# Attention and two MLP layers in one kernel: key and query loads behind the leftover scores, GpSimd's operations behind VectorE's

## The chip, the cores and the metric

The kernel runs on one core of one Trainium2 chip. A core has five engines, each with its own instruction stream, worked off in order: TensorE (PE, matrix products), VectorE (DVE), ScalarE (ACT), GpSimd (POOL) and SyncE (SP), which here issues most of the DMAs. The metric is the device time of one execution, in microseconds (us); less is better.

## The reference

Three stages follow each other. Attention works with sigmoid in place of softmax; its output, with the heads side by side, is the input of a first MLP layer, and that one's output the input of a second, gated one.

```python
def _attn_ref(q, k, v):                     # (4, 12, 448, 64) each
    S = q.shape[2]
    scores = np.matmul(q, k.transpose(0, 1, 3, 2)) / np.sqrt(64) - np.log(S)
    attn = 1.0 / (1.0 + np.exp(-scores))
    return np.matmul(attn, v)

def _moe_ref(x, w_in, w_out):               # x (1792, 768), 768 -> 2048 -> 768
    h = x @ w_in
    return (h - np.tanh(h)) @ w_out

def _moe2_ref(x, w_gate, w_val, w_out):     # 768 -> 1536 -> 768
    gate = 1.0 / (1.0 + np.exp(-(x @ w_gate)))
    return (gate * (x @ w_val)) @ w_out
```

All inputs and the output (1792 x 768) are float32.

## The kernel before

**Attention** goes over 24 pairs of heads (NP = 24). The loop (L3119 and following) makes one iteration per pair p, and in each the engines' instructions are written down in this order:

- `scores(p)`: PE's score products, sa (L2351), from the split keys and queries, each followed by a sigmoid on ScalarE (L2355);
- `split(p + 1)`: six VectorE operations (L2300 to L2309) that split the next pair's keys kt and queries qt into a high and a low part, tile sp; at its end, before the change, `load(p + 4)`, four DMAs of 112 KB from SP (L2266);
- `pair_time()`: a planner fills the other engines' time with work for the MLP layers (below), and issues that work's DMAs on SP;
- `load_v(p + 2)`: the values, one DMA from SP (L2275) and four small ones from GpSimd's own stream (L2277, L2282), tile vt;
- `values(p - 1)`: PE's products of the scores with the values, pv (L2392, L2378), and their eviction to x by ScalarE (L2401); after pairs 5 and 11 a store of x, xs (L2403);
- `rest()`: the leftover scores sl of pair p (L2336), four products per pair that read kt and qt themselves, and their sigmoid al on ScalarE (L2340).

Keys and queries lie in four buffers. `load(p + 4)` writes into the buffer of pair p, whose last reader is `rest()` of pair p, so these DMAs wait for PE's leftover scores. SP issues its DMAs in order over eight semaphores in turn: a DMA is issued only when the one eight places before it has landed.

**The planner.** Weights are loaded as packed integers (st, L1686), decoded by ScalarE and VectorE (mw or ms; the decoding of a part starts with an Abs on ScalarE, L1717, or on VectorE), and some decoded ones are stored for later use (kept, L1795). VectorE, ScalarE and GpSimd convert them into high and low parts (w, w_t, w_b), some of which are stored too (half_t, half_b, L1889). The MLP's matrix products go by a scheme of seven products over sums of blocks; their left operands (a11, s1, s2, a12, s3, s4, a22) are made in attention from the first blocks of x (x0, x1), by casts on VectorE and by sums on both VectorE and GpSimd. All these operations stand on line L1346 in the profile, that of a helper. Each is a task with a due time; the planner goes along with clocks of its own for each engine (`busy`, `now`) and puts each operation of a task on the engine and into the pair where its reckoning ends first. Its time is negative in attention, from -5.38 * 23 = -123.7 to 0. Where it puts an operation on GpSimd at a time over 0, it has it wait for the last VectorE operation that its reckoning ends by then:

```python
            if e == "g" and t > 0:
                before = next((ins for over, ins in reversed(marks) if over < t + 0.05), None)
                if before is not None:
                    tc.add_manual_dep(
                        gpsimd.last.ins, before.ins.name, IN_TURN, reason="shared SBUF port"
                    )
```

`marks` holds the operations that the planner has put on VectorE. The order of instructions on an engine is the order in which they are written; nothing is rearranged afterwards.

**The MLP layers** follow attention on PE: products pa, pb, pc, pe (L2791) of the first layer's first half, then pq (L2497), and so on.

Of the kernel before, what the change touches and what calls it, by code (L numbers as in the profile page):

```python
# [1352 lines left out]
def fast_path(  # L1353
# [134 lines left out]
    class Task:  # L1488
# [66 lines left out]
        def go(self, at):  # L1555
            kinds, f, _, _, lock = self.ops[self.at]
            end, t, e = at
            if e == "s":
                end = moved(t, kinds[e])
                busy[e] = t + 0.4  # L1560
            else:
                busy[e] = end
            if lock:
                busy["l"] = end
            self.end.append(end + SHOW)
            self.at += 1
            if self.done():
                tasks.remove(self)
            elif self.dues:
                self.due = self.dues[self.at]  # L1570
                tasks.sort(key=lambda t: t.due)
            f(ENGINE[e]) if "g" in kinds else f(e) if "a" in kinds and "v" in kinds else f()
            mark(e)
            if e == "g" and t > 0:
                before = next((ins for over, ins in reversed(marks) if over < t + 0.05), None)
                if before is not None:
                    tc.add_manual_dep(
                        gpsimd.last.ins, before.ins.name, IN_TURN, reason="shared SBUF port"
                    )
# [707 lines left out]
    def split(p):  # L2287

        if p >= NP:
            return  # L2290
        qt, kt = qk_t.pop(p)
        t = qkp.tile([128, 2 * KR + QGAP + 2 * S], F32R, tag="sp", name=f"sp{p}", bufs=2)
        kk = t[:, :2 * KR].rearrange("p (i c r) -> p i c r", i=2, r=128)
        qq = t[:, 2 * KR + QGAP:].rearrange("p (i s) -> p i s", i=2)
        parts = (
            (kt[:, :KR - (NCH - 1) * EX].rearrange("p (c r) -> p c r", r=CP), slice(0, CP)),
            (kt[:, (NCH - 1) * CP:KR].rearrange("p (c r) -> p c r", r=EX), slice(CP, 128)),
        )
        for src, r in parts:
            nc.vector.tensor_copy(out=kk[:, 0, :, r], in_=src)  # L2300
        if p == 0:
            nc.scalar.activation(out=qq[:, 0], in_=qt, func=AF.Copy)
        for src, r in parts:
            nc.vector.tensor_tensor(
                out=kk[:, 1, :, r], in0=src, in1=kk[:, 0, :, r].bitcast(F32), op=ALU.subtract
            )
        if p:
            nc.vector.tensor_copy(out=qq[:, 0], in_=qt)
        nc.vector.tensor_tensor(out=qq[:, 1], in0=qt, in1=qq[:, 0].bitcast(F32), op=ALU.subtract)  # L2309
        s_t[p] = kk, qq, kt, qt  # L2310
        load(p + 3)

    slots = [0]

# [781 lines left out]
    with tc.manual_schedule():  # L3096
# [11 lines left out]
        for _ in range(10):  # L3108
            nc.tensor.matmul(pz[:, :S], z[:, :128], z, start=True, stop=True)
        split(0)  # L3110

        first = list(first_jobs)

# [9 lines left out]
        for p in range(NP - 1):  # L3123
            if p == TUNE.get("p0", 2):
                for i, job in enumerate(first):
                    create(job, BEGIN + TUNE.get("c0", 16.0) + gap * (i + 1))
            if p == NP // 2 + 1:
                src_at[0] = now[0] + 6.0
                prepare(0, TUNE.get("x0", -40.0), 6.0)
            rest = scores(p)  # L3130
            split(p + 1)
            pair_time()
            if p:
                load_v(p + 2)
                values(p - 1)
                rest()
        p = NP - 1
        scores(p)
        rest_keys(p - 1)
# [260 lines left out]
```

## Time and profile before

| | |
|---|---|
| time, median of 3 runs | 1067.13 us (1066.64 to 1069.18) |
| the profiled execution | 1068.06 us, of which the span 1066.3 us |
| PE busy | 1043.1 us, 98% of the span |
| VectorE busy | 825.0 us, 77% |
| ScalarE busy | 592.3 us, 56% |
| GpSimd busy | 306.2 us, 29% |
| mean granted clock of PE | 0.993 of full speed |
| DMA engines | 264.56 MB, mean 248 GB/s |

The span runs from the first to the last instruction of one profiled execution; times within the trace count from its start. An operation is named by its output and its input (out<-in, without buffer numbers) and by its line. "Idle before, releaser" in a row of the timeline is the time for which the engine stood before the operation, and what it waited for last. The clock is that which the chip granted to PE, as a share of full speed.

### The profile page before, as it was taken

What the parts mean: (1) busy time and instruction counts of PE and PEld (TensorE: products, weight loads), DVE (VectorE), ACT (ScalarE), POOL (GpSimd) and SP (SyncE); (2) the same over time, 40 slices, a digit from 0 to 9 for tenths busy, and PEclk for the clock granted to TensorE, in tenths of its full rate; (3) what the DMA queues carried; (4) which work ended last, traced back from release to release, by engine and by line L of the source; (5) the groups of instructions that cost most, each with busy time, mean ns of one, the idle gap of its engine ahead of it and who ended that gap; (6) DMA issues with size and microseconds to landing.
All of it is one profiled execution on the core that took longest, in us unless ns stands there. A gap on an engine that the chain in (4) does not pass through costs nothing.

```text
span 1066.3 us, 16297 instructions
## 1 busy us (share of the span) xinstructions
PE 1043.1 (98%) x5913; PEld 937.6 (88%) x5913; DVE 825.0 (77%) x1380; ACT 592.3 (56%) x970; POOL 306.2 (29%) x328
## 2 busy tenths in 40 slices
PE   9989899999999999999999999999999999999996
PEld 5756578989999999999999998999999999999996
DVE  5979997898776899956879999867665888534577
ACT  6756567586467677654677545644334544314343
POOL 5446634524111323121233112352113011016103
PEclk9989999999999999999999999999999999999999
DMA  8998469974463455995557858849777465996312
GB/s 226 272 284 259 130 209 389 374 276 183 159 257 117 186 198 178 334 423 213 219 219 324 317 200 298 333 179 359 269 274 285 179 238 224 395 404 225 133 75 105
DMA packets 63539, 264.56 MB, mean 248 GB/s; under 512 B 8672, under 2 KB 24032, under 8 KB 59360
## 3 DMA queue, kind: packets, MB, share of 16 engines
q1 hardware_dynamic: 59792, 260.40, 66.3%
q0 software_dynamic: 3072, 2.17, 0.9%
q8 instruction: 48, 0.79, 0.3%
q10 hardware_dynamic: 592, 0.92, 0.3%
q14 instruction: 35, 0.29, 0.1%
HBM read 162.40 MB, written 101.06 MB: 247 GB/s over the span
## 4 chain that ended last, share of the span: by engine, by line
PE 90%; DVE 6%; ACT 1%; issue 1%; DMA 1%; POOL 0%; SPq 0%; ACTq 0%; POOLq 0%; DVEq 0%
PE pq L2497 33%; PE pa L2791 13%; PE pb L2791 13%; PE pc L2791 13%; PE pe L2791 7%; PE pv L2392 4%; PE sa L2351 4%; DVE y L1346 1%; PE pv L2378 1%; PE pq_b L2558 1%; PE pq_c L2558 1%; PE sl L2336 1%; PE pq_a L2558 1%; DVE mw L1346 1%; DMA kept<-mw 1%
## 5 line engine op out<-in xcount | busy, mean ns | idle before, releaser
L2497 PE MATMUL pq<-gg,w 128*128 128x448 f32 x1800 | 382.5, 362 | 0.7 <-ACT y L2506 0.7
L2497 PEld LDWEIGHTS pq<-gg,w 128*128 128x128 f32 x1800 | 337.0, 187 | 25.0 <-ACT y L2506 1.1
L1346 DVE TENSOR_TENSOR y<-pq,y 128x448 f32<-128x448 f32 x195 | 120.4, 620 | 57.5 <-PE pq L2497 56.3
L2791 PE MATMUL pa<-a,w_b 128*128 128x448 f32 x720 | 157.3, 362 | 1.0 <-DVE sg L1346 1.0
L2791 PEld LDWEIGHTS pa<-a,w_b 128*128 128x128 f32 x720 | 134.8, 187 | 10.6 <-DVE sg L1346 1.3
L1346 DVE SCALAR_TENSOR_TENSOR mw<-st,mw 128x768 int32<-128x768 int32 x104 | 100.5, 966 | 1.7
L2791 PE MATMUL pc<-s,w_t 128*128 128x448 f32 x360 | 78.7, 362 | 0.2 <-ACT pc L2812 0.2
L2791 PE MATMUL pb<-s,w_t 128*128 128x448 f32 x360 | 78.7, 363 | 0.0
L2791 PE MATMUL pb<-s,w_b 128*128 128x448 f32 x360 | 78.5, 362 | 0.0
L2791 PE MATMUL pe<-s,w_t 128*128 128x448 f32 x360 | 78.5, 362 | 0.0
L2791 PE MATMUL pc<-a,w_t 128*128 128x448 f32 x360 | 78.5, 362 | 0.0
L1346 POOL TENSOR_TENSOR gg<-sg,gg 128x448 fp32r<-128x448 f32 x38 | 43.6, 1159 | 109.8 <-DVE gg L1346 30.3
L1346 POOL TENSOR_TENSOR w<-mw,w 128x384 fp32r<-128x384 f32 x35 | 36.0, 1045 | 131.9 <-ACT w L1869 62.4
L1346 POOL TENSOR_TENSOR w_t<-mw,w_t 128x384 fp32r<-128x384 f32 x37 | 38.1, 1039 | 124.6 <-DVE w_t L1346 45.2
L2355 ACT ACTIVATE at<-sa,bias_s 128x896 f32<-128x896 f32 x72 | 67.2, 1008 | 10.1 <-PE sa L2351 7.8
L2791 PEld LDWEIGHTS pc<-s,w_t 128*128 128x128 f32 x360 | 67.3, 187 | 5.4 <-ACT pc L2812 0.9
L2791 PEld LDWEIGHTS pb<-s,w_t 128*128 128x128 f32 x360 | 67.2, 187 | 5.2 <-issue 0.3
L2791 PEld LDWEIGHTS pb<-s,w_b 128*128 128x128 f32 x360 | 67.5, 187 | 4.5
L2791 PEld LDWEIGHTS pe<-s,w_t 128*128 128x128 f32 x360 | 67.5, 188 | 4.5
L2791 PEld LDWEIGHTS pc<-a,w_t 128*128 128x128 f32 x360 | 67.5, 187 | 4.5
L1346 DVE TENSOR_SCALAR mw<-mw 128x768 f32<-128x768 f32 x104 | 60.4, 581 | 6.4 <-ACT mw L1717 5.0
L2351 PE MATMUL sa<-sp 64*128 64x448 f32 x432 | 52.8, 381 | 10.8 <-ACT al L2340 5.1
(148 smaller groups left out, 1624.2 us busy)
## 6 DMA issues: line engine op xcount, KB each, us to landing
half_t<-w_t SPq DMA_DIRECT2D x40, 768.0 KB, 4.6
w_t<-half_t SPq DMA_DIRECT2D x40, 768.0 KB, 6.7
st<-in_w_out_dram SPq DMA_DIRECT2D x28, 768.0 KB, 6.0
mw<-kept SPq DMA_DIRECT2D x22, 768.0 KB, 5.8
half_b<-w_b SPq DMA_DIRECT2D x20, 768.0 KB, 3.9
w_b<-half_b SPq DMA_DIRECT2D x20, 768.0 KB, 6.3
st<-in_w_in_dram SPq DMA_DIRECT2D x16, 768.0 KB, 6.1
kept<-mw SPq DMA_DIRECT2D x12, 768.0 KB, 4.2
```

What stands on the lines that cost most here:

```text
L1346: self.last = call(*args, **kw)
L2336: nc.tensor.matmul(pl[h * KL:(h + 1) * KL, j, :SH], kt[r, KR:], qt[r, h * SH:(h + 1) * SH], start=True, stop=True,)
L2351: nc.tensor.matmul(pa[:, j, :S], kk[r, ki, c], qq[r, qi], start=(i == 0), stop=(i == 2),)
L2355: nc.scalar.activation(out=at[:, :, c], in_=pa[:, :, :S], func=AF.Sigmoid, bias=bias_s, scale=qk_scale,)
L2378: nc.tensor.matmul(po[j * D:(j + 1) * D, h, :SH], vt[r, j, NCH - 1], al[r, j], start=not last, stop=last,)
L2392: nc.tensor.matmul(po[j * D:(j + 1) * D, h, :SH], vt[:, j, c], at[:, j, c, h * SH:(h + 1) * SH], start=(c == 0 and not rest_first), stop=( ...
L2497: nc.tensor.matmul(po[:, :S], wk[use, j][:, a, d], gt[t][:, c, j], start=i == 0 and not seeded, stop=i == 5, skip_group_check=seeded,)
L2558: nc.tensor.matmul(o, w[:, a, h * KH + d], move[x](b), start=fresh and i == 0, stop=i == 2, skip_group_check=not fresh,)
L2791: nc.tensor.matmul(bank[term], w[:, i, half * KH + c], t[:, j, c], start=fresh and at == 0, stop=at == 3 * KH - 1, skip_group_check=not fresh,
```

## The change

Two things change. First, the loads of keys and queries no longer stand at the end of `split`. `load(3)` comes once after the first split, and `load(p + 4)` at the end of iteration p, behind `rest()`, whose leftover scores free the buffer. Second, the wait of a GpSimd operation for VectorE's operations is now put in at planner times over -100 (TUNE has no entry "gt"), which takes in attention from its fifth pair on.

```diff
--- before.py
+++ after.py
@@ -1571,7 +1571,7 @@
                 tasks.sort(key=lambda t: t.due)
             f(ENGINE[e]) if "g" in kinds else f(e) if "a" in kinds and "v" in kinds else f()
             mark(e)
-            if e == "g" and t > 0:
+            if e == "g" and t > TUNE.get("gt", -100.0):
                 before = next((ins for over, ins in reversed(marks) if over < t + 0.05), None)
                 if before is not None:
                     tc.add_manual_dep(
@@ -2308,7 +2308,6 @@
             nc.vector.tensor_copy(out=qq[:, 0], in_=qt)
         nc.vector.tensor_tensor(out=qq[:, 1], in0=qt, in1=qq[:, 0].bitcast(F32), op=ALU.subtract)
         s_t[p] = kk, qq, kt, qt
-        load(p + 3)
 
     slots = [0]
 
@@ -3108,6 +3107,7 @@
         for _ in range(10):
             nc.tensor.matmul(pz[:, :S], z[:, :128], z, start=True, stop=True)
         split(0)
+        load(3)
 
         first = list(first_jobs)
 
@@ -3134,6 +3134,7 @@
                 load_v(p + 2)
                 values(p - 1)
                 rest()
+            load(p + 4)
         p = NP - 1
         scores(p)
         rest_keys(p - 1)
```

SP is the one engine whose instructions come in another order. Its DMAs around the store of a decoded weight, kept0_1_0, in iterations 9 and 10 (kt13 and qt13 are the keys and queries of pair 13, st00_4 a packed weight, vt11 the values of pair 11), before:

```order
L2266 DMA kt13_858<-in_k_dram 64x448 x2
L2266 DMA qt13_859<-in_q_dram 64x448 x2
L1686 DMA st00_4_866<-in_w_in_dram 128x1536
L2275 DMA vt11_870<-in_v_dram 112x2x192
L2266 DMA kt14_933<-in_k_dram 64x448 x2
L2266 DMA qt14_934<-in_q_dram 64x448 x2
L1795 DMA kept0_1_0_942<-mw0_1_791 128x1536
L1686 DMA st00_5_944<-in_w_in_dram 128x1536
L2275 DMA vt12_950<-in_v_dram 112x2x192
```

and now:

```order
L1686 DMA st00_4_860<-in_w_in_dram 128x1536
L2275 DMA vt11_864<-in_v_dram 112x2x192
L2266 DMA kt13_894<-in_k_dram 64x448 x2
L2266 DMA qt13_895<-in_q_dram 64x448 x2
L1795 DMA kept0_1_0_936<-mw0_1_785 128x1536
L1686 DMA st00_5_938<-in_w_in_dram 128x1536
L2275 DMA vt12_944<-in_v_dram 112x2x192
L2266 DMA kt14_974<-in_k_dram 64x448 x2
L2266 DMA qt14_975<-in_q_dram 64x448 x2
```

In each pair the weight's DMAs and the values now stand ahead of the four loads of keys and queries; pair 14's stand behind kept0_1_0 instead of ahead of it.

GpSimd keeps its order, but its operations get other waits (DVE_49 is a wait for VectorE, Pool_49 one for GpSimd itself, PE_49 one for PE, DMAHW and DMASW ones for landings). Around the values of pair 19, before:

```order
L1346 TENSOR_TENSOR s1_0_1329<-x1_88,s1_0_1329 128x448 [waits DVE_49]
L1346 TENSOR_TENSOR a12_0_1252<-x0_87,a12_0_1252 128x448
L1346 TENSOR_TENSOR a12_0_1252<-x0_87,a12_0_1252 128x448 [waits DVE_49]
L2277 DMA vt19_1489<-in_v_dram 16x3x64 [waits DMAHW5_49,DMASW4_49,PE_49]
L2277 DMA vt19_1489<-in_v_dram 16x3x64 [waits DMASW5_49]
L2282 DMA vt19_1489<-in_v_dram 64x2x64 [waits DMASW6_49]
L2282 DMA vt19_1489<-in_v_dram 64x2x64 [waits DMASW7_49]
L1346 TENSOR_TENSOR x1_88<-x0_87 128x448 [waits Pool_49] x2
L2277 DMA vt20_1564<-in_v_dram 16x3x64 [waits DMAHW4_49,DMASW0_49,PE_49]
```

and now:

```order
L1346 TENSOR_TENSOR s1_0_1323<-x1_88,s1_0_1323 128x448 [waits DVE_49]
L1346 TENSOR_TENSOR a12_0_1246<-x0_87,a12_0_1246 128x448 [waits DVE_49]
L1346 TENSOR_TENSOR a12_0_1246<-x0_87,a12_0_1246 128x448
L2277 DMA vt19_1483<-in_v_dram 16x3x64 [waits DMAHW1_49,DMASW4_49,PE_49]
L2277 DMA vt19_1483<-in_v_dram 16x3x64 [waits DMASW5_49]
L2282 DMA vt19_1483<-in_v_dram 64x2x64 [waits DMASW6_49]
L2282 DMA vt19_1483<-in_v_dram 64x2x64 [waits DMASW7_49]
L1346 TENSOR_TENSOR x1_88<-x0_87 128x448 [waits DVE_49,Pool_49]
L1346 TENSOR_TENSOR x1_88<-x0_87 128x448 [waits Pool_49]
L2277 DMA vt20_1558<-in_v_dram 16x3x64 [waits DMAHW0_49,DMASW0_49,PE_49]
```

The sums x1<-x0 waited for GpSimd's own earlier operations alone; the first of them now also waits for VectorE, for the last weight operation ahead of split 20. The second row's wait is on VectorE's cast of a12 ahead of split 19.

## Rows read from the trace of the kernel before

**Rows 1.** Page, part 1: engine, busy us, share of the span, instructions.
```profile
PE 1043.1 (98%) x5913; PEld 937.6 (88%) x5913; DVE 825.0 (77%) x1380; ACT 592.3 (56%) x970; POOL 306.2 (29%) x328
```

**Rows 2.** Stretches: length, busy us of PE, PEld, DVE, ACT, POOL, PEclk, DMA share, GB/s.
```profile
14.37:67.84 53.47, 53.47 (x585) 37.56 (x580) 47.80 (x101) 38.81 (x50) 25.24 (x41) 1.00 0.91 282
67.84:80.57 12.73, 7.64 (x63) 4.76 (x58) 7.15 (x15) 4.55 (x6) 3.95 (x8) 0.73 0.84 234
...
101.95:111.50 9.55, 7.30 (x63) 4.58 (x59) 9.45 (x13) 3.88 (x5) 8.19 (x11) 0.82 0.64 147
111.50:118.03 6.53, 5.61 (x62) 3.75 (x58) 6.46 (x5) 3.88 (x5) 6.51 (x9) 1.00 0.30 86
118.03:126.12 8.09, 5.70 (x62) 3.78 (x58) 7.92 (x17) 3.88 (x5) 4.07 (x7) 1.00 0.82 220
```

**Rows 3.** Waits, PE, 14 to 166 us: waiter, awaited, total us, times, longest.
```profile
PE sa L2351 <- ACT al L2340: 5.1, 1, 5.1
PE sa L2351 <- DVE sp L2308: 4.5, 2, 2.3
...
PE sa L2351 <- DVE sp L2309: 0.9, 1, 0.9
```

**Rows 4.** Waits, PE, 166 us to the end.
```profile
PE pq_c L2558 <- ACT pq_c L2566: 1.3, 1, 1.3
```

**Rows 5.** Timeline, 58 to 84 us: start, length, engine, line, operation, [idle before, releaser].
```profile
58.48 1.95 DVE L1346 SCALAR_TENSOR_TENSOR mw<-st,mw 128x768 int32<-128x768 int32 x2
...
65.45 1.97 POOL L1346 TENSOR_TENSOR w<-mw,w 128x384 fp32r<-128x384 f32 x2
...
68.25 0.62 DVE L2309 TENSOR_TENSOR sp<-qt,sp 128x448 fp32r<-128x448 f32 x1
...
72.99 0.89 ACT L1717 ACTIVATE ms<-st 128x768 f32<-128x768 f32 x1 [6.23 <-DMA kept<-mw]
...
73.92 1.15 DVE L1346 TENSOR_SCALAR ms<-ms 128x768 f32<-128x768 f32 x2 [5.05 <-ACT ms L1717]
...
83.17 0.61 DVE L2300 CAST sp<-kt 128x336 fp32r<-128x336 f32 x2 [1.69 <-PE sa L2351]
```

**Rows 6.** Chain of waits, 40 to 180 us: start, length, what.
```profile
67.01 5.82 DMA kept<-mw
```

**Rows 7.** Timeline, SP's DMA issues, 44 to 67 us.
```profile
44.69 0.81 SPq L1889 DMA_DIRECT2D half_b<-w_b  x2
...
61.19 1.75 SPq L2266 DMA_DIRECT2D qt<-in_q_dram  x2
...
64.43 1.20 SPq L2266 DMA_DIRECT2D kt<-in_k_dram  x2
65.68 1.24 SPq L2266 DMA_DIRECT2D qt<-in_q_dram  x2
```

**Rows 8.** Timeline, VectorE, 38 us.
```profile
38.45 0.56 DVE L1346 TENSOR_TENSOR w_b<-mw,w_b 128x384 fp32r<-128x384 f32 x1
```

**Rows 9.** Stretch 83.17 to 159.77 us, columns as in rows 2.
```profile
83.17:159.77 76.60, 71.04 (x694) 50.34 (x695) 75.49 (x116) 46.40 (x64) 43.46 (x53) 0.98 0.67 206
```

**Rows 10.** Timeline, VectorE, 160 us.
```profile
160.69 0.63 DVE L1346 TENSOR_TENSOR pe<-pc,p 128x448 f32<-128x448 f32 x1 [0.92 <-PE pc L2791]
```

**Rows 11.** Timeline, 96 to 134 us.
```profile
96.02 4.07 DVE L1346 CAST s<-x 128x448 fp32r<-128x448 f32 x2
...
96.33 3.50 POOL L1346 TENSOR_TENSOR x<-x,x 128x448 f32<-128x448 f32 x3
...
100.84 1.17 POOL L2282 DMA_DIRECT2D vt<-in_v_dram  x2
...
115.19 2.49 PE L2392 MATMUL pv<-at,vt 128*64 128x224 f32 x24
...
133.78 0.39 DVE L1346 CAST s<-x 128x448 fp32r<-128x448 f32 x1
```

**Rows 12.** Tile vt: the landing of its DMAs.
```profile
DMA to landing us min/median/max: 1.8/4.2/8.8
```


## The prediction

> **What bounds the kernel now.** I read the page's busy shares first: TensorE (PE) is busy 98% of the span [rows 1]. So time can only come out of the few places where PE stands, and the next view is the list of PE's waits. After 166 us its largest wait is one of 1.3 us [rows 4]. Before that, in attention, it waits 5.1 us once for a ScalarE result (al, the leftover scores of a pair) and 4.5 + 0.9 us in three places for VectorE's split of the keys and queries (sp) [rows 3]. All that matters here lies in the first 166 us, and since PE hardly waits afterwards, what is saved there comes off the end.
>
> The third view is a table of stretches that begin where PE starts a pair's leftover scores. Ten undisturbed pairs take 53.47 us, 5.35 us each; in four stretches one pair takes 12.73, 9.55, 6.53 and 8.09 us [rows 2]. The losses over 5.35 are 7.38 (pair 11 to 12, **hole A**), 4.20, 1.18 and 2.74 us (pairs 16 to 19, **holes B, C, D**), 15.50 us in all. They exceed the waits because the granted clock, 1.00 in the undisturbed pairs, is 0.73 and 0.82 in A's and B's stretches: of A's 7.38 us, 5.1 are the wait, the other 2.3 come with the lower clock level behind it.
>
> **How hole A comes about.** ScalarE stands 6.23 us until the store of a decoded weight (kept) has landed; only then may it run its Abs into that buffer (ms, L1717). It works in order, so the eviction of pv and the leftover scores stand behind, and PE behind them; VectorE stands 5.05 us for the same Abs [rows 5]. The store is issued at 67.01 us and lands 5.82 us later, at 72.83 [rows 6]. Its data were ready at 58.48 + 1.95 = 60.43 us, when VectorE's last operation on it ended [rows 5]. In between SP worked off key and query loads, up to 65.68 + 1.24 = 66.92 us [rows 7]; the last four of them, pair 14's, stand right ahead of the store.
>
> **The change, first part: the loads.** No instruction is added or removed; on SP four loads per pair go behind the pair's weight transfers and V load. The store thus passes pair 14's four loads, and keeps pair 13's ahead of it. Late bound of its issue: SP's pace stays and only the four loads' own 1.20 + 1.24 us fall away [rows 7], 67.01 - 2.44 = 64.57 us, landing at 70.39 if it still takes 5.82. Early bound: when its data are there, 60.43 us, landing at 66.25. I take about 62, between the two and nearer the early one, because the backlog in which the store stood is older than these four loads: the first two stores of converted halves had their data at 38.45 + 0.56 = 39.01 us [rows 8], yet were issued at 44.69 [rows 7], behind loads that could not start before PE had run the leftover scores of their buffer's pair. With weights ahead of keys those can go out up to 5.7 us sooner, and what queues up behind them shortens. In the old order pair 13's queries, now the last thing ahead of the store, were done at 61.19 + 1.75 = 62.94 us [rows 7]; part of that backlog less makes it 62. Issued at 62, the store lands at 67.8. Any landing up to 67.9 us gives the same: the Abs may not start before GpSimd has read the buffer, 65.45 + 1.97 = 67.42 us, lasts 0.89, and VectorE is not ready for its result before 68.25 + 0.62 = 68.87 us [rows 5].
>
> Then VectorE runs on at 68.87 instead of 73.92 us: 5.05 us. It then stood 1.69 us more at 83.17 us, for PE that hole A had made late [rows 5]; that goes too. Sum for VectorE: 5.05 + 1.69 = **6.74 us**. PE gains 7.38 us in hole A.
>
> What is late next is VectorE. From 83.17 to 159.77 us it is busy 75.49 of 76.60 us [rows 9]; it first waits for PE again at 160.69 - 0.92 = 159.77 us [rows 10], and holes B, C and D are PE waiting for its splits. So PE's extra 7.38 - 6.74 = 0.64 us is given back in hole B, and what reaches the end is VectorE's 6.74 us.
>
> What the moved loads cost: they are needed one split, about three pairs or 16 us, after the scores that free their buffer, so going behind two or three issues of about 0.6 us each (1.20 us for two loads [rows 7]) is hidden. Without that slack it would be at most three issues, 1.8 us a pair.
>
> **The change, second part: the waits.** Sixteen GpSimd operations in attention (sums on x, the low parts of s1 and a12) now start behind the VectorE operation that the planner ends before them, mostly the last one ahead of a split. Beside such operations VectorE does not run: two casts, 0.39 us each alone, took 4.07 us beside three GpSimd sums of 3.50 us, and 2 x 0.39 + 3.50 = 4.28 [rows 11]. The time is lost whole, wherever the sums fall. The waits move it from casts to splits, and the sum of both engines' work up to 159.77 us is unchanged, so I cost this at 0 for the end. Its bounds: a gain of 3.50 us, if one group of three sums came to lie where VectorE stands anyway; a loss of 0.92 us, the slack that VectorE has at 160 us [rows 10], if GpSimd's last group came late.
>
> GpSimd also issues V loads. At 100.84 us two such issues take 1.17 us while VectorE is at work [rows 11]. The Trainium skill, page "SBUF — State Buffer", section "SBUF: two separate sides", calls the two engines' port pair an exclusive lock, as the casts above show it, and adds that a VectorE copy also keeps GpSimd from writing the descriptors of a DMA that it issues; in its example 620 ns become some 3100. That speaks against the waits, which put V issues beside other VectorE work than before. By the page a pair of issues could grow by an estimated 5 us (two of 2.5), more than the lag at which the third rival begins to cost. The row shows nothing of it, and my sum goes by the row.
>
> **Sum.** The profiled execution takes 1068.06 us, 0.93 over the median of 1067.13; I take the gain off the median. 1067.13 - 6.74 = 1060.4 us. With the late bound the Abs starts at 70.39 instead of 72.83, VectorE gains 2.44 us: 1064.7 us. With the waits' gain 6.74 + 3.50: 1056.9; with their loss 1061.3.
>
> **Rivals.**
> First, **all holes close**: the waits put GpSimd's sums where they delay no split that PE waits for. PE's full loss goes, 15.50 us: 1051.6 us. For it: the waits in question are 5.4 us in three places and VectorE only has to be ahead at those. Against: VectorE and GpSimd together would have to get 15.50 - 6.74 = 8.76 us of work out of the stretch, and 1.11 us of VectorE's 76.60 are idle [rows 9]. A chance of 0.1, in-between outcomes included.
>
> Second, **the store is not issued earlier, or lands no earlier**: the DMA engines were 0.91 busy in the stretch before [rows 2], and a transfer issued earlier into a full queue may land when it did. Then PE still waits at pair 12; the gain is between 0 and the late bound's 2.44: 1064.7 to 1067.1 us. For it: a landing of 5.82 us against a data-ready time of 60.43. Against: the loads ahead are moved, not just passed, so the same bytes come behind the store. Chance 0.14; the price includes that the change does nothing.
>
> Third, on the other side, **V comes late**: GpSimd issues four of the five V loads of a pair, in order with its sums. A sum that waits for VectorE holds back the V loads behind it, and then PE waits at pv. In the trace of before V issued by 100.84 + 1.17 = 102.01 us is read at 115.19 [rows 11]; less a landing of 4.2 us [rows 12] and PE's 6.74 us lead that leaves 2.2 us. Pairs 17 to 21 have such sums ahead of their V loads. It starts to cost when GpSimd's queue lags by over 2.2 us, and turns the sign when it exceeds that by 6.74 / 5 = 1.35 us per pair; with 3 us per pair 5 x 3 - 6.74 = 8.3 us slower, 1075.4 us. Against: GpSimd is busy 43.46 of 76.60 us [rows 9], and the VectorE operations that it waits for come earlier too. Chance 0.06.
>
> **How the numbers follow.** The forecast's mechanism, from 1056.9 to 1063.9 us, has 0.7; the first rival 0.1, the second 0.14, the third 0.06. A measurement of this kernel can tell 0.3% (3.2 us) from no change, so faster begins at 1063.9 us: faster 0.7 + 0.1 = 0.8, same 0.14, slower 0.06. The range takes in the forecast's own bounds, the late bound at 1064.7 and part of either neighbour, from 1055.5 to 1065.5 us.
>
> **What would show it.** Right, step one: the store's issue near 61 to 62 us and its landing before 67.9; no wait of over 1 us ahead of the Abs; the stretch from pair 11's to pair 12's leftover scores near 5.35 us; VectorE's split 15 starting near 76.4 instead of 83.17. Right, step two: PE's waits for sp still there, some 6 to 9 us with their clock, but at other pairs between 17 and 23; VectorE busy in nearly all of the time up to PE's first pe chain, which comes some 6.7 us earlier. Wrong: a store issued after 64.6 us; waits of PE for vt; or PE's waits for sp gone, with VectorE idle between 76 and 153 us. The weakest step is that the sum of VectorE's and GpSimd's work decides the end; the second, how early SP reaches the store.

## The result, and the profile after

The changed kernel takes **1058.26 us** (median of 4 runs, 1055.94 to 1059.62), the one before 1068.04 in the runs made with it (1066.64 to 1069.18). The ratio is 0.9907, with a 95% interval of 0.9881 to 0.9932: 9.8 us, 0.9%, faster. The forecast was 1060.4, with a range from 1055.5 to 1065.5. The profiled execution took 1059.62 us, of which the span 1057.7, so the two profiled executions lie 8.44 us apart, and the sums below go by that.

The page's busy shares of after, to be held against [rows 1]:

```profile
PE 1041.7 (98%) x5913; PEld 937.0 (89%) x5913; DVE 816.4 (77%) x1380; ACT 591.8 (56%) x970; POOL 305.4 (29%) x328
```

No engine has more or fewer instructions, yet VectorE is busy 8.6 us less (825.0 - 816.4). That is the first sign that not only idle time went. PE's waits in attention, 12 to 162 us (waiter, awaited, total us, times, longest), against [rows 3]:

```profile
PE sa L2350 <- ACT al L2339: 3.5, 2, 2.6
```

Besides this row the list has only 0.9 us for VectorE's sg and 0.3 us for ScalarE's x. The wait for al fell from 5.1 to 3.5 us. The three waits for VectorE's split, 5.4 us before, are gone. The stretches, columns as in [rows 2]: the first begins and ends with the leftover scores of pairs 11 and 12, the second is the only pair between 78 and 132 us that took more than 5.35 us, and the third runs from VectorE's split 15 to the point at which VectorE first waits for PE's pe, as in [rows 9]:

```profile
67.99:77.86 9.87, 7.23 (x63) 4.47 (x58) 6.92 (x16) 4.54 (x6) 6.05 (x10) 0.83 0.91 214
...
115.30:121.40 6.10, 5.69 (x62) 3.78 (x58) 5.99 (x12) 3.88 (x5) 4.46 (x8) 1.00 0.54 140
80.78:150.99 70.21, 68.84 (x692) 49.38 (x689) 68.12 (x117) 46.02 (x64) 42.57 (x53) 1.00 0.75 216
```

Hole A lost 9.87 - 5.35 = 4.52 us instead of 7.38, so the loads gave less there than the 7.38 forecast. Holes B, C and D together lost 0.75 us instead of 8.12. VectorE's stretch is 70.21 us instead of 76.60, and its busy time in it 68.12 instead of 75.49, for 117 operations against 116. The balance on VectorE: split 15 starts at 80.78 instead of 83.17, **2.39 us** earlier, and the stretch is **6.39 us** shorter. The sum, 8.78 us, is what PE's first pa product gained (139.38 instead of 148.14, 8.76 us), and the rest of the program keeps its length within some 0.2 us.

Why hole A stayed half open, in the timeline of after (start, length, engine, line, operation, [idle before, releaser]):

```profile
26.38 0.61 DVE L2300 CAST sp<-kt 128x336 fp32r<-128x336 f32 x2 [3.20 <-DMA kt<-in_k_dram]
...
60.39 1.95 DVE L1346 SCALAR_TENSOR_TENSOR mw<-st,mw 128x768 int32<-128x768 int32 x2
...
61.37 1.23 SPq L2266 DMA_DIRECT2D qt<-in_q_dram  x2
...
62.69 1.09 SPq L1795 DMA_DIRECT2D kept<-mw  x1
...
67.37 1.98 POOL L1346 TENSOR_TENSOR w<-mw,w 128x384 fp32r<-128x384 f32 x2
...
70.69 0.89 ACT L1717 ACTIVATE ms<-st 128x768 f32<-128x768 f32 x1 [3.78 <-DMA vt<-in_v_dram]
```

and its chain of waits (start, length, what):

```profile
62.69 7.90 DMA kept<-mw
```

The store is issued at 62.69 us, 4.3 us earlier than before, and 0.35 us behind its data, which are ready at 60.39 + 1.95 = 62.34 us. SP's issues of queries ahead of it end at 61.37 + 1.23 = 62.60 us, so at most 0.3 us of SP's backlog is left. But VectorE itself reaches that point 1.91 us later than before (60.39 against 58.48 in [rows 5]), and GpSimd's read of the buffer is later by about the same (67.37 against 65.45). VectorE had stood 3.20 us for a pair's keys at 26 us, where no such wait was before; its wait for a packed weight just ahead of that was 1.72 us instead of 3.58. That the moved loads made it late isn't shown: with the loads at their old place (waits_alone, below) the same operation starts as late, at 60.45 us, without such a wait for keys at 26 us (there it stands 1.14 us for keys at 58 us). The store then took 7.90 us, not 5.82, and landed at 70.59; its issue alone took 1.09 us, against 0.53 in loads_alone. The Abs (ms) followed at 70.69. The row names the last semaphore wait by another transfer, vt; the store's own end, 0.10 us ahead of it, fits better.

### The profile page after: what moved, and what is told of

The parts are those of the page before. It is cut to its first block, busy times and chain, and to the rows that moved or that the text cites. A ratio compares the mean times of both kernels' runs of the same rounds, so it can differ in the third digit from the quotient of the medians.

```text
span 1057.7 us, 16304 instructions
## 1 busy us (share of the span) xinstructions
PE 1041.7 (98%) x5913; PEld 937.0 (89%) x5913; DVE 816.4 (77%) x1380; ACT 591.8 (56%) x970; POOL 305.4 (29%) x328
## 4 chain that ended last, share of the span: by engine, by line
PE 86%; DVE 6%; DMA 4%; issue 1%; ACT 1%; SPq 1%; POOL 0%; ACTq 0%; DVEq 0%; POOLq 0%
PE pq L2496 33%; PE pa L2790 13%; PE pb L2790 13%; PE pc L2790 13%; PE pe L2790 7%; PE pv L2391 2%; PE sa L2350 2%; DVE mw L1346 1%; DMA kt<-in_k_dram 1%; DMA vt<-in_v_dram 1%; DVE y L1346 1%; DMA qt<-in_q_dram 1%; DMA kept<-mw 1%; PE pq_b L2557 1%; PE pq_c L2557 1%
## 5 line engine op out<-in xcount | busy, mean ns | idle before, releaser
L2790 PEld LDWEIGHTS pc<-s,w_t 128*128 128x128 f32 x360 | 67.4, 188 | 5.5 <-ACT pc L2811 1.0
L2948 ACT ACTIVATE gg<-sg 128x896 fp32r<-128x896 f32 x50 | 47.5, 950 | 26.3 <-DVE sg L1346 26.0
```

Source lines behind the costliest of these rows:

```text
L2790: nc.tensor.matmul(bank[term], w[:, i, half * KH + c], t[:, j, c], start=fresh and at == 0, stop=at == 3 * KH - 1, skip_group_check=not fresh,
L2948: h = task.add(dict(a=0.86), lambda: nc.scalar.activation(out=gt_tile(t)[:, 0], in_=sg[t], func=AF.Copy), (), gate_)
```

## The experiments

The loads moved VectorE's start in the stretch, and the waits seemed to shorten its work, against the forecast that they cost and bring nothing. Three explanations were tried for the second part. **Key casts:** VectorE's 128x336 casts of the keys run beside a GpSimd sum, so sums released just ahead of a split cost less. **Values:** a sum that is ready behind GpSimd's DMA issues of the values (V) holds VectorE up already while those issues run, and the waits keep it from being ready. **Neither:** VectorE gains because its inputs come at other times. All kernels are edits of the changed kernel; times are medians, ratios stand to the kernel before of the same chip (1068.52 us, 1069.00, and 1069.01 in the three groups).

### The two parts apart

**loads_alone** keeps the loads' new place and gives the waits back their old bound.

```diff
-            if e == "g" and t > TUNE.get("gt", -100.0):
+            if e == "g" and t > TUNE.get("gt", 0.0):
```

> The loads are moved, GpSimd's operations in attention keep their old waits. Theory 1 (the loads give some 2.7 us in hole A, the new waits the larger rest at holes B to D): the stretch from pair 11's to pair 12's leftover scores near 9.9 us as with the whole change, PE's waits for VectorE's splits at pairs 16 to 19 still there (5 us and more), total 1064 to 1066 us. Theory 2 (that of the prediction: all of the gain comes from the loads, the waits cost and give nothing): 1058 to 1061 us, the waits for the splits gone or moved.

1061.62 us (1061.28 to 1062.59), ratio 0.9935 [0.9918, 0.9952]: 6.9 us faster. The stretches from pair 11 to 12, and from split 15 on (columns as above), and PE's wait for the split:

```profile
67.72:74.86 7.14, 5.62 (x62) 3.68 (x58) 5.82 (x10) 4.55 (x6) 5.92 (x10) 1.00 1.03 267
79.00:153.82 74.82, 69.44 (x680) 49.35 (x677) 73.85 (x117) 45.02 (x63) 43.88 (x52) 0.98 0.66 199
```

```profile
PE sa L2350 <- DVE sp L2308: 4.2, 2, 2.3
```

The total is the forecast's 6.74 us. Its parts are not: split 15 starts 4.17 us earlier (79.00), and the stretch is 1.78 us shorter. Hole A here keeps 1.79 us, its Abs at 69.30 us waiting for GpSimd's read, which ends at 69.26; the store, issued at 63.28 us, had landed by then, 5.7 us after its issue. PE's waits for the split remain.

**waits_alone** keeps the waits and puts the loads back.

```diff
+        load(p + 3)
...
-        load(3)
...
-            load(p + 4)
```

> The loads stay at the end of the split, GpSimd's operations in attention get the new waits. Theory 1: hole A as before (12.7 us from pair 11's to pair 12's leftover scores), but VectorE needs some 70 us instead of 76.6 from its split 15 to its last part of s4, PE's waits for the splits at pairs 16 to 19 nearly gone, total 1061 to 1063 us. Theory 2: VectorE's busy time unchanged at 75 to 76 us in that stretch, total 1067 to 1069 us.

1063.96 us (1062.55 to 1065.73), ratio 0.9955 [0.9939, 0.9972]: 4.6 us faster, from the part that the forecast held at zero.

```profile
69.71:82.93 13.22, 8.24 (x63) 5.05 (x59) 7.83 (x17) 4.54 (x6) 4.05 (x8) 0.74 0.77 219
```

```profile
85.54:157.18 71.64, 69.49 (x694) 49.54 (x695) 70.53 (x116) 46.33 (x64) 43.67 (x53) 1.00 0.70 220
```

Hole A stays whole (the store is issued at 68.68 us, the Abs runs at 74.75), and split 15 is 2.37 us later than before; ahead of hole A PE also stands once for values, 0.88 us up to 61.52 us. But the stretch is 4.96 us shorter, all of it busy time of VectorE (70.53 against 75.49). So the waits do shorten VectorE's work. In this execution (1065.13 us, the second longest of seven) 4.96 - 2.37 = 2.59 us of it reach PE's first pa product. The parts apart add up to 11.5 us, together they give 9.8: they overlap a little, within what the intervals allow.

### Where the waits' gain comes from

**sums_behind_split** lets a GpSimd sum wait for the split's last operation, so that it no longer falls beside the casts of the keys.

```diff
+                if t <= 0 and before is not None:
+                    before = split_end[0]
...
+        split_end[0] = nc.vector.tensor_tensor(
```

> As the whole change, but in attention GpSimd's operations wait for the last operation of the split that is written just ahead of them, not for the last planned operation before the next split, so they begin beside the weight decoding, casts and sums that follow a split. Theory 1, with its mechanism (the sums gain because they begin beside the two key casts of a split, which GpSimd does not block): VectorE's blocked time is back, its stretch from split 15 to the last part of s4 near 74 to 77 us, total 1063 to 1066 us. Rival 3 (any wait that ties the sums to one place behind VectorE's own work gives the same): 1057 to 1060 us.

1058.10 us (1057.71 to 1060.37), ratio 0.9903 [0.9884, 0.9921], as the change itself.

```profile
79.97:150.86 70.89, 69.20 (x692) 49.32 (x689) 69.92 (x117) 46.18 (x64) 46.86 (x53) 1.00 0.73 215
```

VectorE's stretch is 70.89 us, 0.7 more than in the change. Without the key casts beside the sums nearly the whole gain is still there, so they are not what most of it needs. VectorE's busy time there is 1.80 us more than in the change (69.92 against 68.12), so a smaller share can hang on where the sums fall.

**queries_first** writes the split of the queries ahead of that of the keys, so that other operations of VectorE lie beside the sums.

```diff
+        if p:
+            nc.vector.tensor_copy(out=qq[:, 0], in_=qt)
...
+        nc.vector.tensor_tensor(out=qq[:, 1], in0=qt, in1=qq[:, 0].bitcast(F32), op=ALU.subtract)
         for src, r in parts:
             nc.vector.tensor_copy(out=kk[:, 0, :, r], in_=src)
```

> As the whole change, but the split does the queries first, so that the sums begin beside the cast and the subtraction of the queries and the key casts come third. Theory 1 with its mechanism (the two key casts, 0.52 us together, run beside a sum, and the other operations do not): 0.4 to 0.5 us lost at each of seven groups of sums on VectorE, some 3 us in its stretch, total 1059 to 1062 us. Rival 3: no change against the whole change, 1057 to 1060 us, the stretch within 1 us of 70.2.

1058.29 us (1057.47 to 1061.29), ratio 0.9908 [0.9889, 0.9927]. The stretch is 69.62 us. It says little: VectorE now stood for the queries' transfers (11.8 us, seven times, between 12 and 166 us), in part while GpSimd's sums ran, so the two effects cover each other.

**What the rows of before show.** The next view is what VectorE does while GpSimd issues the values' four DMAs, some 2.2 us. First comes an issue behind which the next sum was not ready (it waited for VectorE and began 1.3 us after the issues), then one behind which the next sum began at once, then single rows beside two more of that kind (timeline of before):

```profile
104.20 1.06 POOL L2277 DMA_DIRECT2D vt<-in_v_dram  x2
104.55 0.62 DVE L2309 TENSOR_TENSOR sp<-qt,sp 128x448 fp32r<-128x448 f32 x1
...
107.77 1.21 POOL L1346 TENSOR_TENSOR s<-x,s 128x448 fp32r<-128x448 f32 x1 [1.34 <-DVE s L1346]
...
111.37 1.06 POOL L2277 DMA_DIRECT2D vt<-in_v_dram  x2
111.71 1.62 DVE L2309 TENSOR_TENSOR sp<-qt,sp 128x448 fp32r<-128x448 f32 x1
112.43 1.19 POOL L2282 DMA_DIRECT2D vt<-in_v_dram  x2
...
113.63 1.17 POOL L1346 TENSOR_TENSOR x<-x 128x448 f32<-128x448 f32 x1
...
94.54 1.56 DVE L1346 TENSOR_TENSOR a<-x,a 128x448 fp32r<-128x448 f32 x1
...
117.36 1.32 DVE L1346 CAST a<-x 128x448 fp32r<-128x448 f32 x1
```

The same subtraction (L2309) takes 0.62 us beside the first issue and 1.62 beside the second, 1.00 more. The sum itself starts at 113.63, after that subtraction has ended (111.71 + 1.62 = 113.33), so it is not the sum's run that held it. The row at 94.54 is 0.94 us longer than the 0.62 of its kind, the cast at 117.36 is 0.93 longer than the 0.39 in [rows 11]; both lie beside V issues with a sum that begins as these end (96.33, 118.81). A fourth such case, at 101.38, also overlaps the sum itself. The same place after the change:

```profile
109.00 1.06 POOL L2277 DMA_DIRECT2D vt<-in_v_dram  x2
109.34 0.62 DVE L2309 TENSOR_TENSOR sp<-qt,sp 128x448 fp32r<-128x448 f32 x1
109.88 0.95 DVE L1346 SCALAR_TENSOR_TENSOR ms<-st 128x768 f32<-128x768 f32 x1
110.05 1.50 POOL L2282 DMA_DIRECT2D vt<-in_v_dram  x2
110.86 1.15 DVE L1346 TENSOR_SCALAR ms<-ms 128x768 f32<-128x768 f32 x2
...
113.16 2.49 POOL L1346 TENSOR_TENSOR x<-x 128x448 f32<-128x448 f32 x2 [1.61 <-DVE ms L1346]
```

The sum behind the issue waits for VectorE, and VectorE's operations beside the issue have their own length. Counting V issues from 84 to 145 us whose next sum begins at once (within 0.03 us of their end):

| kernel | such issues | VectorE's stretch | busy in it |
|---|---|---|---|
| before | 4 | 76.60 us | 75.49 us |
| loads_alone | 3 | 74.82 | 73.85 |
| waits_alone | 1 | 71.64 | 70.53 |
| after | 0 | 70.21 | 68.12 |

From four to none the stretch shrinks by 6.39 us, 1.6 us per issue; by that, three would give 75.0 and one 71.8, close to the two kernels between. But 1.6 us is not the price of one hold: the three clean cases show about 1.0 us each. The fourth place mixes two things. Before, VectorE worked on a split beside two GpSimd sums; after, these sums run in part while VectorE stands for keys (rows of before, then of after):

```profile
100.53 2.72 DVE L2304 TENSOR_TENSOR sp<-kt,sp 128x336 fp32r<-128x336 f32 x2
...
102.04 2.22 POOL L1346 TENSOR_TENSOR s<-x,s 128x448 fp32r<-128x448 f32 x2
...
103.17 1.34 DVE L2308 CAST sp<-qt 128x448 fp32r<-128x448 f32 x1
...
99.60 2.34 POOL L1346 TENSOR_TENSOR s<-x,s 128x448 fp32r<-128x448 f32 x2 [0.86 <-DVE s L1346]
...
100.94 0.61 DVE L2300 CAST sp<-kt 128x336 fp32r<-128x336 f32 x2 [1.12 <-DMA kt<-in_k_dram]
101.47 0.95 DVE L2304 TENSOR_TENSOR sp<-kt,sp 128x336 fp32r<-128x336 f32 x2
```

The two subtractions take 0.95 us instead of 2.72 and the cast of the queries 0.38 instead of 1.34: 2.73 us less busy time at this place, against 1.12 us of standing. So part of the gain here is the case that the forecast took as its bound for a gain, sums that fall where VectorE stands anyway. Of the 7.37 us of busy time that went (75.49 - 68.12), the clean cases are 2.87, this place is 2.73, and 1.8 are spread over smaller differences.

**tiny_sum_behind_v** asks whether any sum would do: it puts a sum of 128x8, always ready, behind V's issues of pairs 15 to 21.

```diff
+    tiny = cp.tile([128, 3, 8], F32, tag="tiny", name="tiny")
...
+        if 15 <= p <= 21:
+            nc.gpsimd.tensor_tensor(out=tiny[:, 2], in0=tiny[:, 0], in1=tiny[:, 1], op=ALU.add)
...
+        vector.memset(tiny, 0.0)
```

> As the whole change, but behind GpSimd's four V issues of pairs 15 to 21 stands one small sum of its own (128x8, seven in all, on a tile that nothing else uses) that has nothing to wait for. Theory 4, formed after the four runs before: a GpSimd sum that is ready holds VectorE up already while GpSimd still issues the V loads ahead of it, 2.2 us, besides its own time; the new waits keep it from being ready. Then VectorE loses up to 2.2 us again at each of the seven, its stretch from split 15 to the last part of s4 grows from 70 to 76 us or more, and the total to 1064 to 1072 us. Rival 5: a sum costs VectorE only its own time; seven small ones cost 1 to 2 us of VectorE's, the stretch stays under 73 us, the total 1057 to 1060 us.

1075.53 us (1073.94 to 1076.89), ratio 1.0057 [1.0034, 1.0079], slower than before; but attention has no part in that. VectorE's stretch is 70.37 us, as in the change, and an L2309-like subtraction beside an issue takes 0.68 instead of 0.62 us. So a hold for the whole time of the issues, whatever the sum's length, is refuted. The loss is in the MLP products (PE's lines by form, 160 us to the end, of the changed kernel and of this one: count | busy us, mean ns of one | idle before):

```profile
L2496 PE MATMUL pq<-gg,w 128*128 128x448 f32 x1800 | 382.3, 362 | 0.7 <-ACT y L2505 0.7
```

```profile
L2499 PE MATMUL pq<-gg,w 128*128 128x448 f32 x1800 | 389.6, 366 | 0.7 <-ACT y L2508 0.7
```

The new tile moves what lies behind it by 96 bytes per partition; whether that is the cause was not tried. The total says nothing on the question.

**v_from_sp_old_waits** takes V's issues of pairs 15 to 21 off GpSimd and leaves the waits at their old bound.

```diff
-            if e == "g" and t > TUNE.get("gt", -100.0):
+            if e == "g" and t > TUNE.get("gt", 0.0):
...
+        by = nc.sync if 15 <= p <= 21 else nc.gpsimd
...
-            nc.gpsimd.dma_start(
+            by.dma_start(
```

> The loads are moved, GpSimd's operations have their old waits, and the four small V loads of pairs 15 to 21 are issued by SP instead of GpSimd. Theory 4: with no V issue ahead of a ready sum, VectorE's stretch from split 15 to the last part of s4 falls from 74.8 us (loads alone) to 69 to 72 us without the new waits, total 1056 to 1060 us unless SP's longer queue makes loads late. Rival 5: the stretch stays at 74 to 75 us, total 1060 to 1063 us.

1063.54 us (1061.18 to 1065.76), ratio 0.9948 [0.9929, 0.9968], 1.9 us over loads_alone. The total is against the values theory, but the stretch shows two effects:

```profile
79.46:155.02 75.56, 68.87 (x678) 49.12 (x673) 69.65 (x117) 44.67 (x62) 31.57 (x28) 1.00 0.66 197
```

VectorE is busy 69.65 us, with the same sums at their old waits: 4.20 less than in loads_alone, and near the 68.12 of the change. But it stands 5.9 us in the stretch, 5.0 of them for packed weights (3.4) and keys (1.6) from SP's queue, in which the values now stand too, and PE waits 3.5 us for the split and 1.9 for values. The busy time supports the values theory, the total can't be used.

**half_sum_behind_v** and **half_sum_ahead_of_v** are a pair: the same ready sum of 128x224 on a tile that exists already (so nothing moves in memory, and the output stays as it is), once behind and once ahead of V's issues of pairs 15 to 21.

```diff
         nc.sync.dma_start(out=vt[:CP, :, :NCH - 1], in_=v[p, :, :, :NCH - 1])
+        if 15 <= p <= 21:
+            nc.gpsimd.tensor_tensor(out=scratch, in0=scratch, in1=scratch, op=ALU.add)
...
```

That is the one ahead; the one behind has these two lines after the four issues.

> As the whole change, but behind GpSimd's four V issues of pairs 15 to 21 stands one extra sum (128x224, zeros on a tile that is unused then) that has nothing to wait for. Theory 4, revised: VectorE's operations beside these V issues last longer by about half a us each time, besides the 0.6 us of the sum itself, so VectorE's stretch from split 15 to the last part of s4 is 70.2 + 5 to 9 us. Rival: only the sum's own time, 70.2 + 2 to 4 us, and as much as with the sums ahead of the issues (next run).

> The control of the run before: the same seven extra sums stand ahead of the V issues instead of behind them. Theory 4, revised: no VectorE operation beside a V issue is held up; only the sums' own time, the stretch at 70.2 + 2 to 4 us, 2 us or more below the run before. Rival: the same as the run before within 1 us.

Behind: 1061.43 us (1060.37 to 1061.68), ratio 0.9926 [0.9906, 0.9946]. Ahead: 1059.63 us (1058.69 to 1064.11), ratio 0.9909 [0.9889, 0.9929]. The totals' intervals overlap, and the profiled execution with the sum ahead was the longest of its four, with hole A open; so I go by VectorE's rows and stretch alone. The timeline and the stretch of the kernel with the sum behind:

```profile
88.95 1.06 POOL L2277 DMA_DIRECT2D vt<-in_v_dram  x2
89.29 1.03 DVE L2311 TENSOR_TENSOR sp<-qt,sp 128x448 fp32r<-128x448 f32 x1
90.00 1.17 POOL L2282 DMA_DIRECT2D vt<-in_v_dram  x2
90.24 2.05 DVE L1346 TENSOR_TENSOR a<-x,a 128x448 fp32r<-128x448 f32 x3
91.19 0.61 POOL L2286 TENSOR_TENSOR z<-z 128x224 f32<-128x224 f32 x1
```

```profile
80.14:154.60 74.46, 71.18 (x695) 50.66 (x694) 73.49 (x117) 46.64 (x64) 46.29 (x60) 0.98 0.69 204
```

and of the one with the sum ahead:

```profile
92.99 0.56 POOL L2277 TENSOR_TENSOR z<-z 128x224 f32<-128x224 f32 x1
93.02 0.78 DVE L2310 CAST sp<-qt 128x448 fp32r<-128x448 f32 x1
93.49 1.06 POOL L2279 DMA_DIRECT2D vt<-in_v_dram  x2
93.83 0.63 DVE L2311 TENSOR_TENSOR sp<-qt,sp 128x448 fp32r<-128x448 f32 x1
```

```profile
84.38:156.58 72.20, 69.80 (x695) 49.66 (x696) 70.35 (x116) 46.48 (x64) 46.10 (x59) 1.00 0.73 211
```

With the sum ahead VectorE pays once: the cast beside it takes 0.78 instead of 0.38 us, and the subtraction beside the issues its own 0.63. With the sum behind it pays twice: the subtraction beside the issues takes 1.03 instead of 0.62 while the sum has not begun, and the three operations that lie beside the sum take 2.05 instead of 1.69. The pattern comes back at four of the other pairs: 1.04, 0.92, 1.04 and 0.92 us for that subtraction. The stretch is 4.25 us longer than in the change with the sum behind, short of the 5 to 9 us expected, and 1.99 with it ahead, so by these two executions the place alone is worth 2.26 us for seven half sums, 0.32 us each. With whole sums the extra hold was 1.0 us a time. So it grows with the sum, which fits the tiny sum's 0.06. Why a ready operation behind DMA issues holds the other engine isn't shown.

### Whether the values come late

**sums_wait_for_values** gives the waits their old bound and has GpSimd's first attention operation behind each V load wait for the landing of that load's last DMA.

```diff
+            if e == "g" and t <= 0.0 and v_last[0] is not None:
+                tc.add_manual_dep(gpsimd.last.ins, v_last[0].ins.name, IN_TURN, reason="values landed")
+                v_last[0] = None
+            if e == "g" and t > TUNE.get("gt", 0.0):
```

> The loads are moved, GpSimd's sums have their old waits, and the first sum behind each group of V issues in attention also waits until the last of these V loads has landed; nothing ties it to VectorE. Theory 4, revised after the small sums (a sum that is ready behind V issues holds VectorE up about its own length, 1 us, while the issues still run, and once more when it runs; a sum that has something to wait for does not): VectorE's stretch from split 15 to the last part of s4 falls from 74.8 us (loads alone) to 70 to 72.5 us, total 1057 to 1060 us. Theory 6 (what counts is that the sums come behind a given VectorE operation): the stretch stays at 74 to 76 us, total 1060 to 1064 us.

1072.64 us (1070.36 to 1076.32), ratio 1.0035 [1.0018, 1.0052]: slower than before. The timeline:

```profile
74.96 1.94 POOL L1346 TENSOR_TENSOR w<-mw,w 128x384 fp32r<-128x384 f32 x2 [6.56 <-DMA vt<-in_v_dram]
...
147.68 1.33 DVE L1346 CAST s<-x 128x448 fp32r<-128x448 f32 x1 [6.35 <-POOL x L1346]
```

GpSimd stood 6.56 us ahead of its read of the decoded weight, which kept hole A open to the leftover scores of 84.08 us; VectorE stood 6.35 us for a sum, and PE 5.8 us for values in three places. As a test of what holds VectorE it is spoiled by these waits. It does show what the forecast's third rival would look like: GpSimd's queue late by several us, values late, and a time above that of before. In the change itself no wait of PE for vt is in the list.

### What bounds it next

**keys_ahead_of_values** puts the loads of keys and queries behind the weights' DMAs, but ahead of the values, since VectorE now waits for keys.

```diff
             pair_time()
+            load(p + 4)
             if p:
...
-            load(p + 4)
```

> As the whole change, but the loads of keys and queries stand between the weights and the values, so they pass only the weights. If the lateness of keys in the whole change (VectorE stands 7.6 us for them in attention, 2.3 us before the change) costs time: these waits fall to 2 to 4 us and the total to 1055 to 1057 us. If that waiting is covered by PE: 1057 to 1060 us.

1059.48 us (1058.85 to 1060.73), ratio 0.9914 [0.9896, 0.9933]: no gain over the change. VectorE's waits for keys are 8.6 us instead of 7.6, the one at 25 us still 3.49. The place behind the values is not what makes the keys late.

**abs_on_vector** takes the Abs that waits in hole A off ScalarE, so that the leftover scores need not stand behind it.

```diff
-            if e == "v":
+            if e == "v" or key == (0, 0, 4):
```

> As the whole change, but the one Abs that waits for the store in hole A runs on VectorE (one more operation of 0.95 us there) instead of ScalarE. If what is left of hole A is ScalarE standing in order behind that wait: the stretch from pair 11's to pair 12's leftover scores at 5.4 to 6.5 us instead of 9.9, total 1054 to 1057 us. If VectorE's own lateness takes its place (it now stands for the store, and its splits behind it): PE waits for split 13 or 14 instead, 1057 to 1060 us.

1058.22 us (1055.93 to 1060.02), ratio 0.9896 [0.9877, 0.9916]. Hole A is gone (the leftover scores start at 68.81 and 74.16, 5.35 us apart), and nothing is won: three later pairs, from 100.90 us on, take 5.96, 6.54 and 6.72 us. PE's lead is given back where VectorE can't follow. VectorE's work is the bound, as the forecast had it.

**abs_swapped** therefore also gives ScalarE other Abs operations which the planner had put on VectorE in the second half of attention.

```diff
+            if key == (0, 0, 4):
+                e = "v"
+            elif -60.0 < now[0] < 0.0:
+                e = "a"
             if e == "v":
```

> As the whole change, but the Abs that waits for the store in hole A runs on VectorE, and the four later Abs that the planner had put on VectorE in attention run on ScalarE, so VectorE has 3 x 0.95 us less to do behind pair 12. If VectorE's work still sets the end of attention in the whole change: total 1054 to 1056.5 us. If ScalarE, working in order, then stands for stores and VectorE and holds PE up: 1057 to 1062 us.

**1054.96 us** (1054.66 to 1056.83), ratio 0.9868 [0.9848, 0.9887]: 14.0 us faster than before. The interval just touches that of the change (0.9881 to 0.9932), so that it beats the change is likely rather than shown. Its stretch, VectorE at the stretch's end, and PE's waits in attention:

```profile
81.33:147.55 66.22, 64.57 (x644) 45.70 (x641) 65.39 (x113) 45.89 (x63) 41.88 (x53) 1.00 0.77 228
```

```profile
149.41 0.63 DVE L1346 TENSOR_TENSOR pe<-pc,p 128x448 f32<-128x448 f32 x1 [1.86 <-PE pc L2794]
```

```profile
PE sa L2354 <- DVE sp L2312: 1.0, 2, 0.6
...
PE sa L2354 <- ACT al L2343: 0.8, 1, 0.8
```

Four Abs fewer on VectorE, at 0.95 us each, are 3.8 us. Its stretch is 3.99 us shorter, of which 2.73 us are busy time (65.39 against 68.12) and the rest is less standing, and the first pa product comes 2.53 us earlier than in the change (136.85). VectorE now waits 1.86 us for PE where it waited 0.94, so PE has begun to be the bound again, and about 1 us of the stretch's gain ends there.

## Why the prediction was right, and where not

**The total** was right: 1058.3 against 1060.4, within the range. Two errors of its parts nearly cancelled.

**The store (step one).** "I take about 62" was right (62.69 us), and the reason, SP's backlog, too: it shrank until SP reached the store 0.35 us after its data. The number is in part luck, since the data came at 62.34 us, 1.91 later than the forecast had them. "Issued at 62, the store lands at 67.8" failed: 70.59. The term that was mis-sized is the landing, 7.90 us where the 5.82 of [rows 6] was used; why it took longer isn't settled. GpSimd's read of the buffer was taken at its old time as well: it ended at 67.37 + 1.98 = 69.35 us instead of 67.42, so the Abs could not have started at 67.4 to 67.9 even behind a quick landing. In the kernel with the loads alone the Abs ran at 69.30, held by that read; there the store had landed by then.

**VectorE's 6.74 us.** The runs of the loads alone gave 6.9, but of the 5.95 us by which their VectorE leaves attention earlier, hole A gave 4.17; the other 1.78 came out of the stretch that the forecast took as unchanged, with one held-up operation fewer. In the change hole A gave 2.39. The agreement of the total is in part luck.

**The moved loads, "hidden",** were not quite: VectorE's waits for keys in attention rose from 2.3 us to 7.6 (14 to 160 us), while its waits for packed weights fell from 3.6 to 1.7. PE shows no wait for a split in the change. VectorE was 1.9 us late with the store's data and GpSimd as late with its read, but so they were in waits_alone (60.45 us), where the loads were not moved; what these waits for keys cost isn't shown.

**The waits (step two) are the step that failed.** "The time is lost whole, wherever the sums fall" is true of most sums that run (the casts of the keys are an exception, below). It left out what VectorE loses before the sum runs, while GpSimd still issues V in front of it. The row that would have told it was in the trace of before: the subtraction of 1.62 us at 111.71, beside 0.62 of its kind at 104.55 and in [rows 5]. The forecast went by the sum at 96 us, which lies beside VectorE's casts, and took 100.84 in [rows 11] for the issues' own length, not for what VectorE did beside them. The bound, a gain of 3.50 us, was too small by VectorE's stretch, which lost 4.96 us with the waits alone; the total's gain there, 4.6 us (3.0 to 6.5), doesn't exclude it.

**The rivals.** All holes close: B to D nearly did (0.75 us left), A did not, and where A did (abs_on_vector) VectorE's stretch decided; its objection, that the work doesn't fit in the stretch, fell only because the work itself shrank. The store lands no earlier: it landed 2.24 us earlier than the 72.83 of before, so for hole A this rival, with its bound of 2.44 us, came nearer than the forecast. V comes late: not seen in the change; with the waits alone PE stood 0.88 us for values, once. The rule of the Trainium skill (page "SBUF — State Buffer", section "SBUF: two separate sides") that a VectorE copy keeps GpSimd from writing a DMA's descriptors did not show in its size. Pairs of issues in the stretch of after take 1.03 to 1.17 us, but for three that take 1.49 to 1.50, each with VectorE's TENSOR_SCALAR beside its second half, as at 110.05 us: some 0.3 us more where an estimated 5 had been named. What the runs show is a larger hold on the other side: VectorE's operations take longer while GpSimd issues with a ready sum behind.

**Signs.** Step one: the store's issue was as named; its landing, the wait of 3.78 us ahead of the Abs, and split 15 at 80.78 instead of 76.4 were not. Step two: PE's waits for the split were to stay, at other pairs; they went. I had listed "waits for sp gone, with VectorE idle" as wrong; they went with VectorE busy and with less to do, which I had not listed.

**Open.** The three clean held-up operations account for 1.00 + 0.94 + 0.93 = 2.87 us of the 7.37 of busy time directly; in the fourth place the hold can't be told apart from the sums' own run. The count of issues fits the whole, but four kernels with falling counts are no proof, and they differ in when their inputs come too. What makes the keys late at 26 us, what makes VectorE late at 60 us, and why the store takes 5.7 or 5.8 us in some kernels and 7.9 in the change, was not tried.

## What to carry to other kernels

On an in-order DMA queue, a load that waits for an engine's newest result belongs behind transfers that are ready and on which others wait; then check what the moved load now makes late. When two engines hold each other up, compare one kind of operation at all its places, and look at what the other engine is about to do as well as at what it does; a wait that keeps an operation from being ready can shorten its neighbour. And when a total comes out as forecast, still check the parts: here hole A brought about a third of what was forecast for VectorE, and the part held at zero brought more than that.

## What was not expected of the hardware

- A VectorE subtraction of 0.62 us took 1.62 beside GpSimd's DMA issues when a 1.17 us sum stood ready behind them, and 0.62 when that sum still waited. A half sum (0.56 to 0.61 us) cost 0.3 to 0.4 us there, one of 128x8 0.06.
- The split's casts of the keys (128x336) kept 0.60 us beside GpSimd's sums, as at 118.59 us in the trace of before (a sum from 118.81) and at 105.47 after (0.61, a sum from 105.34), while casts of 128x448 beside sums took 1.3 to 2.8 in the trace of before instead of 0.39. The key casts run at a slower pace to begin with: the larger of the two takes 0.50 us alone for 336 columns, where a cast of 448 takes 0.39.
- With a small tile added, 1800 MLP products took 366 ns each instead of 362, and the kernel's ratio to the one before was 1.0057 instead of 0.9907. The cause was not tried.
